# One fused instruction for norm scaling and mask, a newly planned order, and eight output combinations in a row at the end

## The chip, the cores and the metric

The kernel runs on one core of a Trainium2 chip. The metric is device time in microseconds. A core has five engines that work side by side: TensorE (PE in the profile, its weight loads PEld) for matrix products, VectorE (DVE), ScalarE (ACT) and GpSimd (POOL) for everything else, and SyncE (SP), which here only issues transfers to the 16 DMA engines. Each engine runs its own instructions strictly in program order, so an instruction that waits holds up all behind it on that engine.

## The reference

Attention with a compressive memory feeds a soft mixture of experts (B = H = 8, S = 576, D = 64; 4,608 tokens of width 512; 32 slots, 8 experts):

```
scores = q @ k.T / 8, causal mask;  a = softmax(scores);  local = a @ v
q_p = phi(q)                                     # elu(q) + 1
mem_out = (q_p @ M_prev) / (q_p @ z_prev + 1e-6)
x = g * mem_out + (1 - g) * local                # g = sigmoid(beta), per head
logits = x @ phi;  d = softmax(logits, over tokens);  c = softmax(logits, over slots)
slot_out = relu((d.T @ x) @ w1) @ w2             # per expert
out = c @ slot_out
```

## The kernel before

**Pairs of heads.** Attention runs over 32 pairs (8 batches by 4 pairs of heads, 128 partitions hold two heads). Every step of a pair is a small function `op_*`; the text `SEQ` lists some 2,500 of them as `name@pair` and is the order of the program on all engines at once: each engine gets its instructions in the order in which `SEQ` comes to them. `EV` says for each copy or elementwise step which engine does it (`a` ACT, `v` DVE, `p` POOL). A digit behind a colon names the PSUM bank (`psT0` to `psT3`, or `psS0`, `psS1`) that the step takes; a step that takes a bank waits until the last reader of that bank's content before is done.

**Steps of one pair that the change or the prediction touch.** `s4 s3 s2 s1` are score products into psS (L399), `sa` a small one (L418), `max.*` adds the mask and takes row maxima on DVE (L469), `exp.*` is ACT's exponential (L478), `t.*`, `tf`, `ta` are transposes of the weights into psT (L565, L571, L575), `te.*`, `tfe`, `tae` evict them, `av.*` and `ava` multiply with v (L603, L610), `u4` adds the first block and the memory product (L624 to L629).

**Two round trips through DRAM in every pair.** The softmax sums: `rec` (DVE, L483 and L484) inverts them, `rt` transposes, `rte` copies, `rrw` writes them to DRAM (`rs<-rts`), `rrr` reads them back spread over 64 partitions (`rm<-rs`, two transfers of 144 KB, L504), and `mo` and `xa` (DVE, L643, L654) need them; `mo`, `xm`, `xa` are also the last readers of the three psT banks of the pair's output. The memory norm: `norm` (PE), `neps` scales the 128x144 result out of PSUM, `nmk` multiplies by a 0/1 mask, `nred` sums and inverts (L538), `nrw` and `nrr` go through DRAM (`rb<-rd`), `qn` multiplies q_p by it (L554), and `u4` needs that.

**Weights.** 64 tiles of 512 KB. `w@0` to `w@28` have places of their own and are loaded between pairs; `w@29` to `w@46` go to places that attention frees (`WORD`, `FREE`); the last 17 are loaded over the first ones while the experts run. All transfers but two small ones are issued by SP, in the order of `SEQ`.

**After attention.** The `y` steps finish token 512 of every batch and the slot softmax. `fl.n` are filler products on the identity whose result nobody reads. Then, no longer by `SEQ`, come the experts: `f1` and `f1t` (first layer), `f2(0, ...)` (left half of the output columns), `piece` (a sixteenth of the right half's second layer, 8 PE instructions), `g1` and `g2` (normalise and spread a half), `c1` and `c2` (combination weights of the last two token groups), and `comb(half, group)`: 4 products in two psP buffers (of three), one half evicted by ACT and the other by DVE, and a 512 KB store issued by SP. 18 combinations give the output.

Of the kernel before, what the change touches and what calls it, by code (L numbers as in the profile page):

```python
# [28 lines left out]
loadq@1 qhi@0 kn@0 loadm@0 qlo@0 loadk@1 qrelu@0 kl@0 gate@0 s4@0:01 max.40@0 qexp@0 max.41@0 exp.40@0 qphi@0 fl.2@0:0  # L29
s3@0:0 exp.41@0 s1@0:1 max.30@0 s2@0 norm@0:0 qhi@1 max.20@0 sa@0 max.10@0 t.4b@0:1 neps@0 qlo@1 loadk@2 kn@1 loadm@1  # L30
nmk@0 max.21@0 loadq@2 exp.30@0 loadv@0 max.a@0 kl@1 nred@0 te.4b@0 max.11@0 exp.a@0 nrw@0 max.31@0 exp.21@0 qrelu@1
fl.4@0:2 s4@1:01 exp.20@0 exp.31@0 t.2@0:2 max.41@1 exp.10@0 ta@0:3 t.3@0:0 qexp@1 max.40@1 t.4a@0:1 exp.11@0 tae@0
s3@1:0 qphi@1 te.3@0 te.2@0 nrr@0 s2@1:1 rec@0 te.4a@0 s1@1 rt@0:3 max.10@1 kn@2 qhi@2 t.1@0:0 rte@0 max.11@1 exp.10@1
norm@1:2 rrw@0 kl@2 max.20@1 sa@1 te.1@0 tf@0:1 max.30@1 exp.41@1 loadk@3 av.0@0:3 max.a@1 loadq@3 max.21@1 qlo@2
exp.11@1 neps@1 ava@0:0 exp.40@1 max.31@1 av.1@0 nmk@1 tfe@0 av.3@0 qn@0 s4@2:01 exp.20@1 rrr@0 nred@1 exp.31@1 u4@0:2
max.40@2 exp.21@1 nrw@1 w@0 max.41@2 exp.30@1 av.2@0 loadm@2 qrelu@2 exp.a@1 s3@2:0 loadv@1 rec@1 qexp@2 rt@1:1 s2@2:1
qphi@2 rte@1 exp.41@2 rrw@1 s1@2 xa@0 sa@2 mo@0 kn@3 t.2@1:1 nrr@1 t.3@1:0 max.10@2 qhi@3 te.2@1 t.1@1:3 xm@0 w@1 te.3@1
kl@3 loadq@4 t.4a@1:1 loadk@4 te.1@1 max.31@2 norm@2:2 exp.10@2 max.21@2 t.4b@1:0 te.4a@1 neps@2 rrr@1 qlo@3 tf@1:3
max.a@2 te.4b@1 max.20@2 ta@1:2 max.11@2 av.0@1:1 exp.21@2 max.30@2 nmk@2 tae@1 exp.40@2 nred@2 s4@3:01 exp.a@2 qn@1
nrw@2 exp.20@2 av.3@1 max.41@3 w@2 av.2@1 exp.11@2 ava@1:0 tfe@1 exp.30@2 av.1@1 max.40@3 exp.41@3 u4@1:2 exp.40@3  # L40
s1@3:0 xa@1 qrelu@3 loadm@3 exp.31@2 s3@3:1 loadv@2 max.11@3 nrr@2 exp.11@3 s2@3 rec@2 mo@1 rt@2:3 kn@4 t.3@2:0 max.31@3
t.2@2:1 qhi@4 rte@2 te.3@2 xm@1 t.1@2:3 rrw@2 kl@4 qexp@3 sa@3 ta@2:0 max.20@3 t.4a@2:2 te.1@2 loadk@5 max.21@3 tae@2
t.4b@2:3 te.2@2 qphi@3 tf@2:0 te.4a@2 max.10@3 qlo@4 exp.20@3 norm@3:1 max.30@3 av.0@2:2 exp.10@3 max.a@3 neps@3 rrr@2
exp.31@3 nmk@3 s4@4:01 te.4b@2 qn@2 nred@3 exp.30@3 av.2@2 max.41@4 nrw@3 tfe@2 loadq@5 av.3@2 av.1@2 w@3 max.40@4
exp.a@3 exp.21@3 ava@2:1 u4@2:3 exp.40@4 rec@3 rt@3:0 mo@2 qrelu@4 loadv@3 s1@4:0 rte@3 exp.41@4 s2@4 rrw@3 s3@4:1
max.11@4 xa@2 loadm@4 t.4a@3:0 nrr@3 xm@2 qexp@4 sa@4 ta@3:2 x3.0@0:1 max.10@4 loadk@6 tae@3 max.a@4 tf@3:3 max.20@4
x3e.0@0 t.3@3:2 qhi@5 tfe@3 t.1@3:1 te.4a@3 qlo@5 rrr@3 te.3@3 t.2@3:3 te.1@3 x3.1@0:0 te.2@3 kn@5 t.4b@3:2 qphi@4
av.0@3:1 te.4b@3 kl@5 max.30@4 exp.11@4 loadq@6 ava@3:3 max.31@4 norm@4:2 av.3@3 neps@4 av.2@3 qn@3 exp.a@4 av.1@3
exp.30@4 max.21@4 nmk@4 u4@3:2 exp.20@4 nred@4 exp.31@4 s4@5:01 exp.10@4 mo@3 qrelu@5 loadv@4 loadm@5 exp.21@4 nrw@4
xa@3 t.4b@4:1 max.41@5 x1.0@0:3 te.4b@4 xm@3 qexp@5 t.4a@4:1 max.40@5 ta@4:2 x1.1@0 tae@4 qphi@5 s3@5:0 x1l@0 te.4a@4  # L50
x1m@0 s2@5:1 x3e.1@0 rec@4 nrr@4 s1@5 x1e@0 max.30@5 t.3@4:2 kn@6 max.10@5 rt@4:3 sa@5 te.3@4 x2@0:1 qhi@6 rte@4 t.2@4:0
x2a@0 exp.10@5 rrw@4 max.20@5 t.1@4:3 qlo@6 te.2@4 max.11@5 tf@4:2 max.31@5 te.1@4 loadk@7 x4.0@0:0 loadq@7 tfe@4 x2m@0
kl@6 w@4 norm@5:3 exp.41@5 ava@4:2 neps@5 av.0@4:1 max.21@5 exp.31@5 x4a.0@0 x3.2@0:3 nmk@5 exp.40@5 rrr@4 max.a@5
nred@5 x3.3@0:0 x3e.2@0 s4@6:01 qn@4 nrw@5 exp.30@5 x3e.3@0 exp.11@5 u4@4:3 max.40@6 exp.21@5 exp.a@5 av.1@4 qrelu@6
exp.20@5 loadm@6 w@5 max.41@6 qexp@6 av.2@4 av.3@4 exp.41@6 qphi@6 s1@6:0 loadv@5 s2@6 nrr@5 rec@5 x2e@0 s3@6:1 mo@4
rt@5:0 xa@4 qhi@7 sa@6 t.1@5:1 rte@5 xm@4 t.3@5:2 kn@7 rrw@5 te.1@5 max.31@6 ta@5:0 t.2@5:3 te.3@5 kl@7 max.11@6 loadk@8
t.4a@5:1 te.2@5 max.10@6 loadq@8 t.4b@5:2 max.21@6 te.4a@5 tf@5:3 max.30@6 te.4b@5 qlo@7 norm@6:1 max.20@6 exp.11@6
av.0@5:2 max.a@6 exp.20@6 tae@5 neps@6 rrr@5 exp.30@6 nmk@6 s4@7:01 qn@5 nred@6 exp.10@6 exp.31@6 tfe@5 av.2@5 nrw@6
ava@5:0 exp.21@6 max.40@7 av.1@5 exp.40@6 max.41@7 av.3@5 u4@5:1 exp.a@6 x2s@0 exp.41@7 s1@7:0 qrelu@7 rec@6 loadv@6
exp.40@7 s3@7:1 loadm@7 max.11@7 mo@5 exp.11@7 s2@7 nrr@6 rt@6:3 xa@5 kn@8 t.1@6:2 xm@5 t.2@6:0 qhi@8 rte@6 te.1@6  # L60
t.4a@6:3 rrw@6 max.31@7 te.2@6 qlo@8 ta@6:1 sa@7 max.10@7 t.3@6:2 qexp@7 tae@6 loadk@9 max.21@7 tf@6:0 w@6 te.4a@6
max.a@7 t.4b@6:1 qphi@7 te.3@6 x4.1@0:3 te.4b@6 max.20@7 norm@7:2 exp.10@7 max.30@7 av.0@6:1 tfe@6 rrr@6 kl@8 exp.30@7
x5@0:0 neps@7 s4@8:01 x4a.1@0 exp.31@7 nmk@7 x5e@0 qn@6 nred@7 exp.a@7 av.1@6 exp.21@7 max.41@8 nrw@7 exp.20@7 ava@6:2
loadq@9 av.3@6 max.40@8 av.2@6 u4@6:3 rec@7 exp.40@8 rt@7:0 mo@6 qrelu@8 loadm@8 s2@8:0 rte@7 loadv@7 rrw@7 xa@6 s3@8:1
s1@8 nrr@7 t.3@7:0 max.10@8 xm@6 qexp@8 t.2@7:1 t.4a@7:2 te.3@7 max.21@8 sa@8 max.11@8 x3.0@1:3 te.2@7 te.4a@7 tf@7:0
x3e.0@1 t.1@7:1 qphi@8 rrr@7 tfe@7 t.4b@7:2 max.31@8 te.1@7 w@7 x3.1@1:3 loadq@10 kn@9 max.a@8 ta@7:0 max.30@8 av.0@7:1
x3e.1@1 te.4b@7 kl@9 qhi@9 norm@8:3 exp.11@8 av.1@7 neps@8 qn@7 exp.10@8 av.3@7 av.2@7 tae@7 nmk@8 max.20@8 exp.31@8
u4@7:23 qlo@9 nred@8 exp.20@8 nrw@8 exp.41@8 ava@7 w@8 mo@7 qrelu@9 s4@9:01 loadk@10 exp.21@8 loadv@8 xa@7 loadm@9
exp.30@8 xm@7 x1.0@1:0 max.41@9 x1.1@1 t.4b@8:1 max.40@9 x1l@1 exp.a@8 t.4a@8:3 qexp@9 x1m@1 ta@8:2 nrr@8 s2@9:0 qphi@9
x1e@1 w@9 s1@9 rec@8 te.4a@8 s3@9:1 max.20@9 tae@8 te.4b@8 rt@8:0 x1d@0 x2@1:3 max.11@9 kn@10 tf@8:2 qhi@10 rte@8 x2m@1  # L70
t.1@8:1 rrw@8 kl@10 exp.11@9 x2a@1 t.3@8:0 max.30@9 te.1@8 t.2@8:3 max.21@9 te.3@8 sa@9 qlo@10 max.10@9 norm@9:1 te.2@8
max.31@9 x4.0@1:0 exp.41@9 neps@9 av.0@8:3 max.a@9 nmk@9 exp.10@9 qn@8 exp.30@9 rrr@8 x3.3@1:1 nred@9 tfe@8 s4@10:01
x3e.3@1 exp.40@9 nrw@9 w@10 u4@8:21 loadk@11 max.41@10 exp.31@9 loadq@11 x4a.0@1 exp.20@9 av.2@8 max.40@10 loadm@10
exp.a@9 av.3@8 x2e@1 ava@8 qrelu@10 exp.21@9 av.1@8 qexp@10 rec@9 sa@10:0 x3.2@1:0 loadv@9 exp.40@10 qphi@10 nrr@9
s1@10:1 x3e.2@1 mo@8 s3@10 s2@10 xm@8 rt@9:0 kn@11 t.4a@9:3 max.a@10 rte@9 max.21@10 t.2@9:2 rrw@9 te.4a@9 max.20@10
t.3@9:0 qhi@11 te.2@9 max.30@10 norm@10:3 qlo@11 loadq@12 te.3@9 xa@8 t.1@9:2 loadk@12 exp.a@10 neps@10 w@11 tf@9:0
max.10@10 te.1@9 max.11@10 t.4b@9:1 kl@11 max.31@10 exp.41@10 ta@9:3 av.0@9:2 te.4b@9 exp.31@10 rrr@9 tae@9 nmk@10 tfe@9
exp.11@10 s4@11:01 qn@9 exp.30@10 nred@10 ava@9:1 exp.10@10 max.40@11 av.1@9 nrw@10 exp.20@10 max.41@11 av.3@9 av.2@9
exp.21@10 x2s@1 u4@9:3 exp.40@11 exp.41@11 rec@10 s1@11:0 qrelu@11 loadv@10 s3@11:1 loadm@11 max.11@11 mo@9 exp.11@11
s2@11 nrr@10 ta@10:0 xa@9 kn@12 sa@11 t.4a@10:2 xm@9 qhi@12 tae@10 rt@10:1 qexp@11 t.1@10:0 max.30@11 qlo@12 tf@10:3  # L80
rte@10 te.1@10 max.a@11 max.31@11 rrw@10 t.3@10:1 te.4a@10 t.2@10:0 max.20@11 te.3@10 qphi@11 t.4b@10:2 loadk@13 te.2@10
x4.1@1:1 kl@12 tfe@10 norm@11:0 exp.20@11 max.21@11 av.0@10:3 exp.31@11 max.10@11 neps@11 rrr@10 x1d@1 s4@12:01
exp.21@11 te.4b@10 nmk@11 qn@10 exp.10@11 x4a.1@1 ava@10:0 exp.30@11 nred@11 av.2@10 av.3@10 max.41@12 exp.a@11 av.1@10
# [1050 lines left out]
```

## Time and profile before

| | |
|---|---|
| time, median of 3 runs | 452.92 us (452.63 to 454.46) |
| profiled execution, its own time | 454.92 us |
| its span (first to last instruction) | 453.1 us |
| mean granted TensorE clock | 0.984 |
| PE, DVE, ACT, POOL busy | 426.6, 344.5, 333.0, 152.9 us |
| moved by DMA | 97.42 MB, mean 215 GB/s |

The busy time of an engine is an average over stages with different limits. An idle time of PE is read together with what ended it: the profile names the engine, line and tile that released the waiting instruction, and from there one goes back along that engine to the transfer or instruction that was late.

### The profile page before, as it was taken

How to read it: one execution, taken by the hardware profiler on the slowest of the kernel's cores; microseconds unless marked ns; L12 is line 12 of the kernel's file. 1: busy time of each engine (PE TensorE's matmuls, PEld its weight loads, DVE VectorE, ACT ScalarE, POOL GpSimd, SP SyncE). 2: the span in 40 equal slices, each digit the busy share in tenths (PEclk: the TensorE clock that was granted, in tenths of full speed). 3: DMA queues.
4: the chain of work that ended last, by engine and by line, in shares of the span. 5: the costliest groups of instructions: out<-in, count | busy, mean ns of one | idle time of the engine just before them, and what ended most of it. 6: DMA issues, size and time to landing. Idle time of an engine off the chain costs nothing.

```text
span 453.1 us, 12442 instructions
## 1 busy us (share of the span) xinstructions
PE 426.6 (94%) x4364; PEld 283.2 (62%) x4364; DVE 344.5 (76%) x1200; ACT 333.0 (73%) x947; POOL 152.9 (34%) x165
## 2 busy tenths in 40 slices
...
GB/s 157 146 251 196 195 117 248 163 214 247 225 194 193 215 161 208 214 196 169 273 185 220 159 157 232 153 139 201 186 169 128 89 317 297 352 359 412 243 327 291
DMA packets 65710, 97.42 MB, mean 215 GB/s; under 512 B 14704, under 2 KB 41072, under 8 KB 65648
## 3 DMA queue, kind: packets, MB, share of 16 engines
...
q10 hardware_dynamic: 288, 0.09, 0.1%
...
## 4 chain that ended last, share of the span: by engine, by line
PE 67%; DVE 12%; DMA 9%; ACT 5%; issue 3%; POOL 1%; SPq 1%; DVEq 0%; ACTq 0%; POOLq 0%
PE psS L399 12%; PE psT L603 12%; PE psT L565 12%; DMA rm<-rs 7%; PE psT L624 5%; DVE P L469 4%; PE psT L727 4%; PE pf L966 3%; PE pf L949 3%; PE pp L1011 2%; PE psT L571 2%; PE psT L522 2%; ACT P L478 2%; ACT at L333 2%; PE psT L666 2%
## 5 line engine op out<-in xcount | busy, mean ns | idle before, releaser
L478 ACT ACTIVATE P<-P,nm 128x320 f32<-128x320 f32 (+4 forms) x288 | 166.2, 587 | 9.4 <-DVE nm L469 8.7
L469 DVE CUSTOM_DVE_ANT_0 P<-psS,mq 128x192 f32<-128x192 f32 (+3 forms) x256 | 133.6, 548 | 11.0 <-PE psS L399 9.8
L333 ACT COPY at<-psT 128x512 f32<-128x512 f32 (+1 forms) x187 | 94.4, 553 | 29.1 <-PE psT L565 10.3
L565 PE MATMUL psT<-cs,P 128*128 128x128 f32 x640 | 89.0, 281 | 4.5 <-DVE xt L654 2.5
L399 PE MATMUL psS<-K,X 64*128 64x288 f32 (+3 forms) x960 | 88.3, 319 | 4.1 <-DVE nm L469 3.2
L399 PEld LDWEIGHTS psS<-K,X 64*128 64x128 f32 x960 | 69.2, 185 | 26.0 <-issue 7.5
L603 PE MATMUL psT<-at,mq 128*64 128x256 f32 (+3 forms) x512 | 83.5, 443 | 0.6 <-ACT P L478 0.4
L565 PEld LDWEIGHTS psT<-cs,P 128*128 128x128 f32 x640 | 72.9, 144 | 10.4 <-issue 5.5
L478 ACT ACTIVATION_READ_ACCUMULATOR P<-P,nm 128x1 f32 x288 | 57.3, 199 | 0.0
L385 POOL TENSOR_TENSOR X<-mq,X 128x512 fp32r<-128x512 f32 x31 | 40.8, 1315 | 24.2 <-DVE X L336 10.7
L391 POOL TENSOR_TENSOR K<-kq,K 128x576 fp32r<-128x576 f32 x27 | 38.6, 1429 | 10.1 <-DVE nm L469 5.3
L603 PEld LDWEIGHTS psT<-at,mq 128*64 128x64 f32 x512 | 28.9, 136 | 18.4 <-issue 9.5
L624 PE MATMUL psT<-kq,m 64*64 64x512 f32 x64 | 34.2, 614 | 0.9 <-POOL kq L554 0.8
L643 DVE TENSOR_TENSOR xt<-psT,rm 128x448 f32<-128x448 f32 (+7 forms) x60 | 23.8, 435 | 13.8 <-DMA rm<-rs 7.8
L625 PE MATMUL psT<-at,mq 64*64 64x512 f32 x64 | 34.2, 615 | 0.0
L627 PE MATMUL psT<-kq,m 64*64 64x512 f32 x64 | 34.2, 615 | 0.0
L626 PE MATMUL psT<-at,mq 64*64 64x512 f32 x64 | 34.2, 615 | 0.0
L338 POOL TENSOR_SCALAR X<-mq 128x512 fp32r<-128x512 f32 x21 | 13.0, 619 | 52.9 <-PE psT L489 20.9
L336 DVE COPY at<-psT 128x512 f32<-128x512 f32 (+2 forms) x45 | 25.0, 563 | 4.5 <-PE psT L565 3.1
L338 POOL TENSOR_SCALAR K<-kq 128x576 fp32r<-128x576 f32 x17 | 11.7, 691 | 48.3 <-PE psS L399 39.6
L509 POOL TENSOR_SCALAR kq<-mq 128x576 f32<-128x576 f32 x22 | 14.8, 674 | 39.0 <-PE psT L629 36.5
L516 DVE SCALAR_TENSOR_TENSOR kq<-mq,kq 128x576 f32<-128x576 f32 x32 | 26.0, 814 | 2.3 <-ACT mq L512 2.2
(198 smaller groups left out, 686.7 us busy)
## 6 DMA issues: line engine op xcount, KB each, us to landing
...
```

The source lines that it names most:

```text
L333: nc.scalar.copy(o, i)
L385: ALU_ENG[ev("qlo", n)].tensor_tensor(out=X[:, 1, :], in0=st[n]["q"][:, 64:576], in1=X[:, 0, :].bitcast(F32), op=ALU.subtract)
L391: ALU_ENG[ev("kl", n)].tensor_tensor(out=K2[:, 1, :], in0=st[n]["k"][:, 0:S], in1=K2[:, 0, :].bitcast(F32), op=ALU.subtract)
L399: nc.tensor.matmul(out(h), X[ROW[h], x, 128 * i - 128:128 * i], K2[ROW[h], y, o + k0:o + k1], start=(x, y) == (0, 0), stop=(x, y) == (0, 1))
L469: nc.vector.tensor_tensor_reduce(out=sm, in0=src, in1=msk, op0=ALU.add, op1=ALU.min, scale=-0.125, scalar=3.0e38, accum_out=s["nm"][:, J:J ...
L478: nc.scalar.activation(sm, sm, AF.Exp, scale=-1.0, bias=s["nm"][:, J:J + 1], accum_out=s["sum"][:, J:J + 1])
L565: nc.tensor.transpose(out=ps[:, 256 * x + 128 * h:256 * x + 128 * h + 128], in_=chunk(n, i, h, c), identity=ident)
L603: nc.tensor.matmul(s["oa"][ROW[h], 512 - w:512], vt[:, c, ROW[h]], at[:, base + 512 * h:base + 512 * h + w], start=first, stop=s["parts"] ...
L624: nc.tensor.matmul(om[ROW[0], :], s["m"][ROW[0], 0:64], s["qp"][ROW[0], 64:576], start=True, stop=True)
L625: nc.tensor.matmul(w2(s["oa"][ROW[1], :]), vt[ROW[0], 4, ROW[1]], af[ROW[0]], start=first, stop=s["parts"] == 5)
L626: nc.tensor.matmul(w2(s["oa"][ROW[0], :]), vt[ROW[1], 4, ROW[0]], af[ROW[1]], start=first, stop=s["parts"] == 5)
L627: nc.tensor.matmul(om[ROW[1], :], s["m"][ROW[1], 0:64], s["qp"][ROW[1], 64:576], start=True, stop=True)
```

## The change

Three things change.

1. **Norm.** `nmk` is gone. Its mask and the gate factor are multiplied once at the start into a small table `mg`, and `neps` becomes one DVE instruction for all 32 pairs that adds 1e-6 and multiplies by `mg`. Before, `neps` was on ACT in 12 pairs and on DVE in 20, `nmk` on POOL in 24 and on DVE in 8.
2. **Order.** `SEQ`, `EV` and `WORD` are new throughout. Beside it `EV` moves seven evictions of 512 columns from DVE to ACT, POOL takes five casts `qhi` more, and the fillers shrink from 13 units (`fl.2 fl.4 fl.5 fl.1 fl.1`) to 7 (`fl.2 fl.1 fl.2 fl.1 fl.1`).
3. **Last phase.** `c1` and `c2` move up between the first-layer products; `comb(0, 0)` to `comb(0, 7)` stand in a row, then 13 pieces in a row, then `comb(0, 8)`.

```
     def op_neps(n):
         rn = st[n]["rn"] = sml.tile([128, 144], F32, name="rn", bufs=1)
-        if ev("neps", n) == "a":
-            nc.scalar.activation(rn, st[n]["nps"][:, 0:144], AF.Identity, bias=epg[:, n % NP:n % NP + 1], scale=gc[:, n % NP, 9:10])
-        else:
-            nc.vector.tensor_scalar(out=rn, in0=st[n]["nps"][:, 0:144], scalar1=1e-6, scalar2=gc[:, n % NP, 9:10], op0=ALU.add, op1=ALU.mult)
-    def op_nmk(n):
-        rn = st[n]["rn"].rearrange("a (u x) -> a u x", x=9)
-        ALU_ENG[ev("nmk", n)].tensor_tensor(out=rn, in0=rn, in1=maskn.rearrange("a (u o) -> a u o", o=1).broadcast_to([128, 16, 9]), op=ALU.mult)
+        nc.vector.scalar_tensor_tensor(out=rn.rearrange("a (u x) -> a u x", x=9), in0=st[n]["nps"][:, 0:144].rearrange("a (u x) -> a u x", x=9), scalar=1e-6,
+                                       in1=mg[:, n % NP].rearrange("a (u o) -> a u o", o=1).broadcast_to([128, 16, 9]), op0=ALU.add, op1=ALU.mult)
...
     f1(0, 0)
     f1(0, 1)
     f1t(0, 0)
+    c1(7)
     f1(1, 0)
     f1t(0, 1)
+    c1(8)
     f1(1, 1)
     f1t(1, 0)
+    c2(7)
     f2(0, 0, 0)
     f1t(1, 1)
+    c2(8)
...
     g2(0)
-    c1(7)
     piece(1)
-    comb(0, 0)
-    comb(0, 1)
-    c1(8)
-    piece(2)
-    comb(0, 2)
...
-    comb(0, 6)
-    piece(3)
+    for t4 in range(NQ - 1):
+        comb(0, t4)
+    piece(13)
     g1(1)
-    comb(0, 7)
+    comb(0, NQ - 1)
     g2(1)
-    comb(0, 8)
```

SP's queue early in attention, before: what stands ahead of and behind the `rm<-rs` of pair 1 (`w_` tiles are weights, `mq<-in_q` and `kq<-in_k` the inputs of pair 4, `mq<-in_v` values, `rb<-rd` the norm's way back).

```order
L499 DMA rs<-rts 4x128 x2
L500 DMA rs<-rts 2x1x64
L550 DMA rb<-rd 64x4x144 x2
L769 DMA w_474<-in_w_dram 128x1024
L361 DMA mq<-in_q_dram 128x704
L366 DMA kq_103<-in_k_dram 128x640
L504 DMA rm<-rs 64x576 x2
L544 DMA rd<-rq 128x9
L769 DMA w_552<-in_w_dram 128x1024
```

The same place now:

```order
L493 DMA rs<-rts 4x128 x2
L494 DMA rs<-rts 2x1x64
L537 DMA rb<-rd 64x4x144 x2
L355 DMA mq<-in_q_dram 128x704
L498 DMA rm<-rs 64x576 x2
L360 DMA kq_103<-in_k_dram 128x640
L531 DMA rd<-rq 128x9
```

The weight ahead of this transfer and the one behind it are gone from here (the first weight now comes in pair 3), and the k load stands behind it.

SP's queue around the `rm<-rs` of pair 17, before:

```order
L366 DMA kq_103<-in_k_dram 128x640
L769 DMA w_3482<-in_w_dram 128x1024
L361 DMA mq<-in_q_dram 128x704
L504 DMA rm<-rs 64x576 x2
L544 DMA rd<-rq 128x9
L769 DMA w_3549<-in_w_dram 128x1024
L769 DMA w_3551<-in_w_dram 128x1024
```

Around that of pair 20, now:

```order
L355 DMA mq<-in_q_dram 128x704
L360 DMA kq_104<-in_k_dram 128x640
L756 DMA w_4040<-in_w_dram 128x1024
L498 DMA rm<-rs 64x576 x2
L531 DMA rd<-rq 128x9
L756 DMA w_4098<-in_w_dram 128x1024
L756 DMA w_4101<-in_w_dram 128x1024
```

In the new order pair 17 has no weight just ahead of its `rm<-rs`, and pair 20 has the set that pair 17 had: one weight, one q and one k load ahead, two weights behind.

PE at the last pair, before: the products with v, five filler units on `cs` (the identity; each row of `x5` is five units), then `u4`.

```order
L603 MATMUL psT_6053<-at,mq 64x512 x2
L610 MATMUL psT_6061<-at,mq 64x64 x2
L603 MATMUL psT_6053<-at,mq 64x384 x2
L355 MATMUL psS_6070<-cs 128x256 x5
L624 MATMUL psT_6076<-kq_104,m 64x512
```

And now:

```order
L590 MATMUL psT_6020<-at,mq 64x512 x2
L597 MATMUL psT_6028<-at,mq 64x64 x2
L590 MATMUL psT_6020<-at,mq 64x384 x2
L590 MATMUL psT_6020<-at,mq 64x128 x2
L349 MATMUL psS_6038<-cs 128x256 x2
L611 MATMUL psT_6041<-kq_104,m 64x512
```

Two filler units are left of five, and one more product with v stands ahead of them.

## Rows read from the trace of the kernel before

**Rows 1.** The page, part 1: busy us, share of the span, instructions.

```profile
PE 426.6 (94%) x4364; PEld 283.2 (62%) x4364; DVE 344.5 (76%) x1200; ACT 333.0 (73%) x947; POOL 152.9 (34%) x165
```

**Rows 2.** Stretches: start:end, us, busy of each engine (instructions), PEclk, DMA share, GB/s.

```profile
0.00:46.00 46.00, 39.53 (x328) 25.89 (x330) 32.96 (x120) 35.51 (x99) 18.03 (x25) 1.00 0.63 188
46.00:356.00 310.00, 304.52 (x3118) 210.39 (x3118) 272.11 (x978) 264.56 (x768) 130.90 (x138) 0.99 0.65 190
356.00:394.00 38.00, 34.74 (x378) 24.41 (x378) 20.79 (x67) 18.52 (x54) 4.00 (x5) 0.96 0.80 276
394.00:420.00 26.00, 25.87 (x303) 10.93 (x298) 3.83 (x7) 2.85 (x6) 0.00 (x0) 1.00 0.99 381
420.00:453.00 33.00, 21.91 (x253) 11.58 (x253) 14.81 (x29) 11.58 (x23) 0.00 (x0) 0.88 0.84 291
```

**Rows 3.** Timeline of PE: start, us, instruction, [idle before <-releaser].

```profile
34.98 0.64 PE L624 MATMUL psT<-kq,m 64*64 64x512 f32 x1 [0.77 <-POOL kq L554]
...
39.54 0.70 PE L399 MATMUL psS<-K,X 64*128 64x320 f32 x6 [2.22 <-DVE nm L469]
...
222.34 0.63 PE L565 MATMUL psT<-cs,P 128*128 128x128 f32 x4 [1.34 <-DVE xt L643]
...
372.11 0.63 PE L565 MATMUL psT<-cs,P 128*128 128x128 f32 x4 [2.55 <-DVE xt L654]
```

**Rows 4.** Timeline of DVE: first uses of the spread softmax sums.

```profile
38.73 0.23 DVE L654 TENSOR_TENSOR xt<-psT,rm 128x64 f32<-128x64 f32 x1 [3.99 <-DMA rm<-rs]
...
186.05 0.76 DVE L643 TENSOR_TENSOR xt<-psT,rm 128x256 f32<-128x256 f32 x2 [1.42 <-DMA rm<-rs]
...
221.43 0.76 DVE L643 TENSOR_TENSOR xt<-psT,rm 128x192 f32<-128x192 f32 x2 [1.40 <-DMA rm<-rs]
```

**Rows 5.** Timeline of SP: issues of transfers (start, us spent issuing).

```profile
30.64 2.19 SPq L504 DMA_DIRECT2D rm<-rs  x2
...
180.15 1.14 SPq L504 DMA_DIRECT2D rm<-rs  x2
...
214.65 1.12 SPq L504 DMA_DIRECT2D rm<-rs  x2
...
363.65 1.51 SPq L504 DMA_DIRECT2D rm<-rs  x2
...
436.65 0.37 SPq L1013 DMA_DIRECT2D out_dram<-P  x1
```

**Rows 6.** Stretches behind the wait at 222, columns as in group 2.

```profile
223.00:226.50 3.50, 3.50 (x20) 3.46 (x19) 3.50 (x13) 2.55 (x5) 0.23 (x1) 0.53 0.52 111
```

**Rows 7.** Groups of DVE, ACT and POOL: xcount | busy us, mean ns | idle before us <-releasers.

```profile
L538 DVE TENSOR_REDUCE rq<-rn 128x9 f32<-128x144 f32 x32 | 13.5, 421 | 8.1 <-POOL rn L534 8.0
L529 DVE TENSOR_SCALAR rn<-psT,rm 128x144 f32<-128x144 f32 x20 | 7.3, 363 | 1.0 <-PE psT L522 0.8
...
L534 DVE TENSOR_TENSOR rn<-rn,rm 128x144 f32<-128x144 f32 x8 | 2.4, 303 | 0.0
```

**Rows 8.** Timeline of PE and DVE ahead of the last pair's u4.

```profile
378.45 0.76 DVE L554 TENSOR_TENSOR kq<-kq,rb 128x576 f32<-128x576 f32 x1 [2.30 <-DMA rb<-rd]
...
379.72 2.43 PE L355 MATMUL psS<-cs 128*128 128x256 f32 x10
```

**Rows 9.** Timeline of PE in the last phase (L966 products, L1011 combinations).

```profile
430.94 1.50 PE L966 MATMUL pf<-w,at 128*32 128x256 f32 x24
...
436.64 2.69 PE L1011 MATMUL pp<-xk,cT 32*128 32x256 f32 x24 [0.30 <-DVE P L336]
439.52 2.69 PE L1011 MATMUL pp<-xk,cT 32*128 32x256 f32 x24 [0.19 <-DVE P L336]
```

**Rows 10.** Stretches of the last phase, columns as in group 2.

```profile
422.00:434.00 12.00, 11.99 (x163) 5.54 (x163) 6.65 (x14) 4.37 (x10) 0.00 (x0) 1.00 0.87 300
434.00:438.00 4.00, 3.40 (x36) 2.07 (x34) 2.42 (x4) 2.42 (x6) 0.00 (x0) 1.00 0.85 294
438.00:451.00 13.00, 4.77 (x44) 3.00 (x44) 4.21 (x7) 3.50 (x6) 0.00 (x0) 0.77 1.04 360
```

433 lines of the change are left out of this document (209 added, 224 removed).

## The prediction

> **What bounds the kernel now.** I read the page first, then a table of stretches, then the waits of PE, and from each wait back to what was late. The page says that PE is busy 94% of the span and DVE 76% [rows 1]. The stretches say where [rows 2]. In the long middle of attention, 46 to 356 us, PE is busy 304.5 of 310 us and DVE 272.1: PE sets the pace, DVE comes behind it with 12% to spare, ACT is like DVE, and POOL is busy for less than half. The start (0 to 46) loses 6.5 us of PE, and the end of attention (356 to 394) 3.3. The experts (394 to 420) keep PE full. In the last 33 us PE is idle for 11, and the DMA engines write: 360 GB/s from 438 on [rows 10].
>
> So a change of the order is worth what it does to PE's few idle times, and to nothing else in attention. The large ones stand in the timeline [rows 3]: 0.77 and 2.22 us near 35 and 39, 1.34 at 222, 2.55 at 372. The last two and the 2.22 have one cause, which DVE's timeline shows [rows 4]: DVE stands 3.99 us at 38.7 and 1.40 at 221.4 for `rm<-rs`, the way back of the softmax sums. While it waits, the row maxima behind it are not taken, or the psT banks of the finished pair are not free, and PE stands. The reader should see how long that way back takes from its issue to its first use: 30.64 to 38.73 is 8.1 us, 214.65 to 221.43 is 6.8, and 180.15 to 186.05 is 5.9 [rows 4, 5]. The third has one weight tile of 512 KB just ahead of it in SP's queue and costs PE almost nothing; the first two have one ahead and one or two behind, with inputs among them. The last one (363.65 to the end of PE's wait at 372.11) has two weights just ahead of it.
>
> **The change part by part.**
>
> *Norm.* Twelve `neps` come to DVE at 0.363 us (the old DVE form, which also reads PSUM), eight `nmk` of 0.303 leave it [rows 7]: 4.4 less 2.4, DVE gains 1.9 us of work in all. The new form has no row; it is nearest to the old `neps`, since both write 144 columns from PSUM. Its bounds are nothing more than that row and 0.67, both old instructions together: 32 x 0.3 = 10 us more on DVE. The seven evictions that move to ACT take more off DVE than the norm adds. What `nmk` cost as a wait stands in the sum's row: DVE was idle 8.0 us for POOL's `rn` [rows 7]. I cost all this at nothing: in the middle PE covers it, being busy 304.5 of 310 while DVE has 38 us free [rows 2]. Without that cover it is between 8.0 less 1.9, a gain of 6.1, and a loss of 10. A gain is capped too: PE's idle time in the middle is 5.5 us.
>
> *The order at pair 1.* The weight ahead of `rm<-rs` and the one behind go, and the k load moves behind it; what is left is lighter than at 180.15, where 5.9 us were enough. I take the waits of 0.77 (for `qn`, whose `rb<-rd` shares that queue) and 2.22 as gone: -3.0 us. Bounds: nothing gained if only the place moves, and -4 if DVE's whole 3.99 counts.
>
> *Pairs 17 and 20.* Pair 17's wait cost 1.34 us, and behind it the granted clock is 0.53 over 3.5 us, mostly 1.2 GHz where it had been 2.4 [rows 3, 6]; at half speed that is some 1.65 us of work lost, together 3.0. In the new order pair 17 has no weight just ahead. But pair 20 has exactly pair 17's set: k, q and a weight ahead, two weights behind, and on PE almost the same products stand between its `rrr` and the bank that `mo` frees (scores, products with v, `u4`; one small `sa` more). I take 3.0 away and put 3.0 back: 0, bounds -3.0 and +1 (pair 8 has a weight, k and q ahead as well and a little less work to cover them).
>
> *The end of attention.* Pair 30 now has three weights ahead of its `rm<-rs`, not two, and the third waits for a place that the transposes of the pair free. Behind `rrr` PE has less to do than before: a `t` (0.63 us for four transposes [rows 3]) and an `x4` of eight products, which I take alike, have moved ahead of it. So 2.55 us grow by some 1.2: +1.2, bounds 0 (if the queue moves faster) and +3.
>
> *Fillers.* Five units before the last `u4` took 2.43 us, and `qn`, for which they might bridge, had ended at 379.2, before they began [rows 8]. Three of five go: -1.5 us, if `qn` is as early again; bounds 0 and -2. The others that go stand at the start, where PE waits for DVE anyway.
>
> *Last phase.* In 422 to 434 PE is busy 11.99 of 12.00, so combinations among pieces hide their evictions; in a row (434 to 438) it is busy 3.40 of 4.00 [rows 10], and three combinations take 2.88 us, start to start [rows 9]. Eight in a row are 7.7 us, 15% of it waits: 1.2 us lost. A piece takes 0.50 (24 instructions in 1.50 [rows 9]) and 13 of them 6.5, as before. `g2`'s copy on ACT, some 0.4 us, is no longer covered by a combination. The four transposes of `c1` and `c2` only move. So the first right-hand store, issued at 436.65 [rows 5], comes up to 1.6 later. For the end it is the queue that counts: 3.6 and 1.2 MB are moved from 422 to 438 [rows 10], 9 of the 18 stores of 0.52 MB, and the other nine take 13 us at 360 GB/s. In the new order the first eight are fed at one per 0.96 us, sooner than 360 GB/s takes them (1.46 each), so they are out by 434; then the queue runs dry while 13 pieces run, and nine stores are left at about 438.2. So +0.3. Bounds: +1.6, and -2.7 if the queue never ran dry (16 us at 360 GB/s are 5.8 MB and not 4.8).
>
> **The sum.** -3.0 + 0 + 1.2 - 1.5 + 0.3 = -3.0 us. The profiled execution took 454.92 us, 453.1 of it span, and lies 2.0 above the median of the runs, 452.92; I carry the difference over: 449.9 us.
>
> **The rivals.**
>
> *The stalls are not put back.* The new order spaces transfers so that neither pair 20 nor pair 30 waits longer than the third case above: -3.0 more at pair 20. For it: weights are now absent from the first pairs and the queue's mean is 190 GB/s in the middle [rows 2]. Against: those weights must come somewhere, and pairs 8, 13, 14 and 20 now hold one or two. 446.9 us, chance 0.18.
>
> *Clock.* PE gets six filler units less, and a further stretch at 1.2 GHz follows, at the end of attention or when the experts begin: 1.65 us each by the same step as at pair 17, 451.6 us with one. For it: after 1.34 us of waiting the clock did fall [rows 3, 6]. Against: after the waits of 0.77 and 2.22 near 35 it did not, the mean over 0 to 46 is 1.00 [rows 2]. Chance 0.13. The Trainium skill, TensorE: Matmul & The Clock Gate, Part 1, says that the throttled state is the default and that activity releases it, which speaks against taking products away that keep PE busy; the trace agrees in the fall behind pair 17, and no row shows a fall for want of fillers.
>
> *No change.* PE sets the pace, and a new order with the same products finds new waits for those removed: the sum's gain of 3.0 at pair 1 comes back at other pairs, say 3.0 at pair 22, which has a weight and a k load ahead and two us of work less to cover them than now. 452.9 us, chance 0.18.
>
> *Slower: DVE waits for the norm product.* `neps` now stands on DVE in all pairs, ahead of row maxima that free the score banks. Where it comes up before PE has done `norm`, maxima and then PE wait. The old `neps` on DVE waited 1.0 us in 20 [rows 7], 0.05 each, which speaks against it; that ACT took twelve of them speaks for it, since ACT's wait held up no maximum. At 0.25 us a pair it costs 8.0, and the sum becomes +5.0: 457.9 us. It turns the sign at 0.09 a pair and is slower by half a per cent from 0.17. Chance 0.16.
>
> **How the numbers follow.** The forecast has 0.35, the rivals 0.18, 0.13, 0.18 and 0.16. Half a per cent, about what a measurement of this kernel can tell from no change, is 2.3 us: 450.7 and 455.2 are the limits. The forecast's own range, from its bounds taken one at a time, is 447 to 452; three quarters of it lie below 450.7. Faster: 0.18 + 0.26 and a little of the clock's case, 0.47. Slower: 0.16 and some of the no-change case, 0.20. Same: the rest, 0.33. The range reaches from 446, a little below the first rival, to 455.5, which leaves out most of the last.
>
> **What would show it.** In the changed kernel's profile: no wait of DVE over 1.5 us for `rm<-rs` before 50 us, and PE idle less than 3 us in total in the first 46; a wait of some 1.4 us at pair 20, near 255, with the clock at 0.5 behind it, and none at pair 17; a wait over 3 us before the last pair's transposes; DVE's wait for `rn` gone and its wait before `neps` not above 2 us in 32; f1 beginning some 3 us earlier than at 394; 8 combinations in about 7.7 us, a hole in the stores before the right half, and the time from the first f1 to the end the same within 0.5. The prediction is wrong if the middle changes by more than 3 us, which none of its terms explains, or if the last phase gains because the queue does not run dry.

## The result: slower by 1.1%

The changed kernel took 458.69 us in the median of five executions (456.69 to 461.53), beside 454.46 (452.63 to 454.86) for five of the kernel before on the same chip. The ratio is 1.0114, 95% interval 1.0066 to 1.0162: slower, by less than 2% but clear of no change, where 449.9 was forecast. Ratios here and below leave out disturbed executions, so a ratio can differ from the quotient of two medians, which are over all. The profiled execution of the changed kernel took 460.05 us, span 458.1.

### The profile page after: what moved, and what is told of

Its sections match the earlier page's. It is cut to its first block, busy times and chain, and to the rows that moved or that the text cites. A ratio compares the mean times of both kernels' runs of the same rounds, so it can differ in the third digit from the quotient of the medians.

```text
span 458.1 us, 12415 instructions
## 1 busy us (share of the span) xinstructions
PE 424.2 (93%) x4352; PEld 280.6 (61%) x4352; DVE 341.7 (75%) x1195; ACT 331.3 (72%) x937; POOL 148.2 (32%) x148
## 4 chain that ended last, share of the span: by engine, by line
PE 63%; DMA 16%; DVE 13%; ACT 3%; issue 2%; SPq 1%; POOL 1%; DVEq 0%; ACTq 0%; POOLq 0%
PE psT L590 12%; PE psS L393 11%; PE psT L552 11%; DMA rm<-rs 8%; PE psT L611 5%; DVE P L463 4%; PE pf L953 3%; PE pf L936 3%; PE psT L714 3%; DMA rs<-rts 2%; PE pp L998 2%; PE psT L558 2%; DMA rd<-rq 2%; PE psT L516 2%; DVE xt L630 2%
## 5 line engine op out<-in xcount | busy, mean ns | idle before, releaser
L472 ACT ACTIVATE P<-P,nm 128x448 f32<-128x448 f32 (+4 forms) x288 | 166.0, 582 | 9.7 <-DVE nm L463 7.9
L326 ACT COPY at<-psT 128x512 f32<-128x512 f32 (+1 forms) x193 | 97.6, 554 | 34.1 <-PE psT L552 22.5
L590 PE MATMUL psT<-at,mq 128*64 128x128 f32 (+3 forms) x512 | 82.9, 442 | 0.0
L472 ACT ACTIVATION_READ_ACCUMULATOR P<-P,nm 128x1 f32 x288 | 55.8, 194 | 0.0
L385 POOL TENSOR_TENSOR K<-kq,K 128x576 fp32r<-128x576 f32 x27 | 40.1, 1486 | 17.9 <-ACT K L326 8.7
L379 POOL TENSOR_TENSOR X<-mq,X 128x512 fp32r<-128x512 f32 x29 | 39.1, 1348 | 13.6 <-DVE at L329 6.6
L331 POOL TENSOR_SCALAR X<-mq 128x512 fp32r<-128x512 f32 x26 | 16.3, 625 | 69.8 <-PE psS L393 24.1
L503 POOL TENSOR_SCALAR kq<-mq 128x576 f32<-128x576 f32 x24 | 16.2, 673 | 53.6 <-PE psT L616 50.7
L541 POOL TENSOR_TENSOR kq<-kq,rb 128x576 f32<-128x576 f32 x16 | 23.5, 1471 | 19.4 <-DMA rb<-rd 16.1
L331 POOL TENSOR_SCALAR K<-kq 128x576 fp32r<-128x576 f32 x19 | 13.2, 695 | 47.3 <-PE psS L393 35.2
```

The lines of the kernel that those rows point to most:

```text
L326: nc.scalar.copy(o, i)
L379: ALU_ENG[ev("qlo", n)].tensor_tensor(out=X[:, 1, :], in0=st[n]["q"][:, 64:576], in1=X[:, 0, :].bitcast(F32), op=ALU.subtract)
L385: ALU_ENG[ev("kl", n)].tensor_tensor(out=K2[:, 1, :], in0=st[n]["k"][:, 0:S], in1=K2[:, 0, :].bitcast(F32), op=ALU.subtract)
L472: nc.scalar.activation(sm, sm, AF.Exp, scale=-1.0, bias=s["nm"][:, J:J + 1], accum_out=s["sum"][:, J:J + 1])
L590: nc.tensor.matmul(s["oa"][ROW[h], 512 - w:512], vt[:, c, ROW[h]], at[:, base + 512 * h:base + 512 * h + w], start=first, stop=s["parts"] ...
```

## The profile after

First part of the page, then the stretches (start:end, us, busy time of each engine, PEclk, DMA share, GB/s). Line numbers are those of the changed kernel, 6 to 13 less than before; in the experiments they are each kernel's own.

```profile
PE 424.2 (93%) x4352; PEld 280.6 (61%) x4352; DVE 341.7 (75%) x1195; ACT 331.3 (72%) x937; POOL 148.2 (32%) x148
0.00:46.00 46.00, 41.25 (x346) 26.74 (x346) 34.99 (x125) 35.92 (x101) 20.34 (x25) 1.00 0.56 160
46.00:356.00 310.00, 297.31 (x3055) 204.31 (x3051) 263.93 (x953) 258.50 (x746) 120.61 (x117) 1.00 0.67 192
356.00:396.00 40.00, 35.60 (x388) 24.83 (x391) 22.98 (x78) 22.32 (x64) 6.20 (x6) 0.96 0.75 246
396.00:422.00 26.00, 26.00 (x298) 11.64 (x294) 6.91 (x22) 3.43 (x8) 1.06 (x1) 1.00 1.00 396
422.00:458.00 36.00, 24.09 (x288) 13.12 (x280) 12.94 (x20) 11.08 (x20) 0.00 (x0) 0.88 0.85 286
```

Against [rows 2]: PE did 1.7 us more in the first 46 us, so the start did get better. Then it was idle for 12.7 us of the 310 in the middle, where it had been idle for 5.5: 7.2 lost. The timeline of PE shows at which waits:

```profile
29.52 0.63 PE L552 MATMUL psT<-cs,P 128*128 128x128 f32 x4 [1.01 <-DVE xt L642]
...
50.04 0.63 PE L552 MATMUL psT<-cs,P 128*128 128x128 f32 x4 [0.97 <-DVE xt L630]
...
76.99 0.28 PE L483 MATMUL psT<-cs,r 128*9 128x128 f32 x1 [1.62 <-DVE r L478]
...
79.38 0.33 PE L552 MATMUL psT<-cs,P 128*128 128x128 f32 x1 [0.80 <-DVE xt L634]
...
181.33 0.27 PE L562 MATMUL psT<-cs,P 128*64 128x128 f32 x1 [2.19 <-DVE xt L641]
...
194.25 0.98 PE L552 MATMUL psT<-cs,P 128*128 128x128 f32 x7 [0.61 <-DVE xt L634]
...
377.20 0.65 PE L552 MATMUL psT<-cs,P 128*128 128x128 f32 x4 [3.03 <-DVE xt L630]
```

These belong to pairs 0, 2, 4 (two), 13, 14 and 30. Those of pairs 2 to 14 are 6.2 of the 12.7 us; the rest is in waits of 0.84 at most, for copies, casts, row maxima and M. None was among the waits of before [rows 3] but the last, and pair 17's 1.34 is gone. Behind most stands the way back of the softmax sums, as before. (The first weight comes earlier than the section on the change says: it is issued at 41.40, between pair 2's write at 39.92 and its read at 42.88.) DVE's timeline at pairs 4 and 13, and what SP issued at pair 13:

```profile
75.02 0.23 DVE L641 TENSOR_TENSOR xt<-psT,rm 128x64 f32<-128x64 f32 x1 [1.68 <-DMA rm<-rs]
...
180.43 0.76 DVE L630 TENSOR_TENSOR xt<-psT,rm 128x256 f32<-128x256 f32 x2 [2.92 <-DMA rm<-rs]
```

```profile
167.95 0.60 SPq L493 DMA_DIRECT2D rs<-rts  x2
168.60 0.60 SPq L494 DMA_DIRECT2D rs<-rts  x1
169.30 1.29 SPq L537 DMA_DIRECT2D rb<-rd  x2
170.63 1.08 SPq L756 DMA_DIRECT2D w<-in_w_dram  x2
171.82 0.36 SPq L355 DMA_DIRECT2D mq<-in_q_dram  x1
172.28 1.11 SPq L498 DMA_DIRECT2D rm<-rs  x2
```

At pair 13 two weights and a q load stand ahead of the read: 8.1 us from 172.28 to the first use, as at pair 1 before [rows 4, 5], and 12.5 from the write's issue. At pair 4 no weight stands there and the read took 4.8 us or less, yet DVE waited 1.68: in this order it comes to the use 3.2 us behind the issue.

A single execution can mislead here. `old_last` (below) runs the same attention again, and its profile says which waits come back: PE stands 1.11 us at pair 4, 1.81 at pair 13 and 2.73 at pair 30. Pair 14's does not, and pair 8, with two weights near its way, costs 1.77 in its place.

The clock, the norm and the last phase, by windows and by group:

```profile
223.00:227.00 4.00, 4.00 (x44) 2.79 (x41) 3.75 (x17) 3.69 (x12) 1.41 (x3) 1.00 0.99 340
377.00:381.50 4.50, 4.30 (x24) 4.27 (x24) 2.10 (x6) 1.17 (x2) 0.00 (x0) 0.62 0.42 151
L520 DVE SCALAR_TENSOR_TENSOR rn<-psT,rm 128x144 f32<-128x144 f32 x32 | 9.6, 302 | 4.2 <-PE psT L516 4.1
426.00:434.00 8.00, 7.32 (x84) 4.16 (x88) 4.75 (x8) 3.93 (x7) 0.00 (x0) 1.00 0.86 292
398.40:458.10 59.70, 47.69 (x553) 22.94 (x552) 18.56 (x37) 14.51 (x28) 0.00 (x0) 0.93 0.91 329
```

The stretch at half speed near 223 [rows 6] is gone, one behind the last long wait remains (0.50 from 373.4 to 376.8 us before). The new norm takes 0.302 us and waits 4.2 us in 32 for its product. From the first f1 to the end pass 59.7 us, beside 59.3.

So the loss is made in attention: the last score product ends at 365.22 (361.14 before), f1 begins at 398.41 (393.87). For these two executions the account closes: 1.7 won up to 46 us, 7.2 lost in the middle, of which 1.65 comes back with the half-clock stretch that went, makes 3.9 of the 4.1; the end of attention adds 0.5 and the last phase 0.5. In three more profiles of the old order (`last_only`, `fl_only`, `norm_only`) the last score product ends at 359.4 to 361.9, in one more of the new (`old_last`) at 363.1, so in these six the new order is always later, by 1.2 to 5.9 us.

## The experiments

Medians are over all executions of a kernel; "before" in the same calls had 454.0 to 455.5.

**Which part of the change.** `norm_only`: before, with the one-instruction norm and no `nmk`.

```diff
-        nc.vector.tensor_scalar(out=rn, in0=..., scalar1=1e-6, scalar2=gc[...], op0=ALU.add, op1=ALU.mult)   # or ACT; then nmk
+        nc.vector.scalar_tensor_tensor(out=rn..., in0=..., scalar=1e-6, in1=mg[...], op0=ALU.add, op1=ALU.mult)
```

> The order and the last phase of before; only the norm is changed: the masked scaling in one DVE instruction that reads PSUM, no nmk, all 32 neps on DVE. Theory Q (queue: the changed kernel lost its time because loads stand ahead of rm<-rs at other pairs than before, so the norm costs nothing): within 1.5 us of before, DVE's wait for the norm product below 3 us in 32. Theory N (norm: DVE stands for the norm product with row maxima behind it): 3 to 5 us slower than before, with a wait of DVE before neps of 4 us or more in all. The prediction's term was 0, with bounds -6.1 and +10.

Measured: 454.81, ratio 1.000 (0.9964 to 1.0037). DVE waited 4.0 us for the product, more than theory Q's 3 and as much as theory N asked for, and it cost nothing. Theory N falls in the order of before.

`last_only`: before, with the changed last phase (the part of the diff behind `SEQ`).

> The order and the norm of before; only the last phase is changed (both transposes of the last combination weights ahead, eight left combinations in a row, 13 pieces, the ninth behind). Prediction's term: +0.3 us (bounds +1.6 and -2.7), first f1 to the end of the span within 0.5 us of before's 59.3. Theories Q and N say nothing against it. A rival: the hole in the stores costs as much as the nine stores run sooner, +1.5 us or more.

Measured: 454.51, ratio 1.001 (0.998 to 1.004), 59.7 us from f1 to the end. The term holds as far as it can be told: with the old last phase this stretch took 59.3 to 60.1 us in ten profiles, 59.6 on average, with the new one 59.7 to 59.9 in eight, 59.8 on average (the two kernels without weights left out).

`old_last`: the changed kernel with the last phase of before.

> The changed kernel with the last phase of before: the new order and the new norm alone. If the loss is in attention (Q, N, or the order of computation, theory C), 457 to 459 us, as the changed kernel; if the last phase were the cause, 453 to 454.

Measured: 459.92 (453.16 to 465.67), ratio 1.0057 (1.0014 to 1.0101). The loss is there without the new last phase: all of it by the medians, half by the ratio, whose interval overlaps that of the whole change. With `norm_only` and `last_only` at no change, that points at the order.

**What in the order: the queue ahead of the read?** `loads_behind`:

```diff
- ... rrw@13 nrr@13 w@13 w@14 loadq@16 rrr@13 nrw@14 ...
+ ... rrw@13 nrr@13 rrr@13 w@13 w@14 loadq@16 nrw@14 ...
```

> The changed kernel; in pairs 0 to 30 each load of q, k or a weight that stood between the two ways of the softmax sums (write rs<-rts, read rm<-rs) is put just behind the read; nothing else moves. Theory Q: the ways from issue to first use fall to 4.5 us or less in all pairs, DVE's idle time for rm<-rs falls from 9.2 us to below 4, the waits of PE at pairs 13 and 14 (2.19 and 0.61) go, and the time falls by 3 us or more, to 452 to 455. Theories N and C (the order of the instructions on PE, DVE and POOL): the ways get shorter but the time stays within 1.5 us of the changed kernel's 458.7. It can also get slower if a load that comes later is then waited for (q or k of the next pairs).

Measured: 461.45, ratio 1.0129 (1.0084 to 1.0174): no gain, and theory Q in this simple form falls. PE's waits at pairs 13, 14 and 30 for `xt` went, as Q said. But what was put behind the read stood ahead of the next pair's M, v and write, and PE now waited for the first two (timeline of PE):

```profile
126.15 0.45 PE L508 MATMUL psT<-kq,m 128*32 128x144 f32 x8 [1.45 <-DMA m<-in_M_dram]
...
384.39 1.08 PE L582 MATMUL psT<-at,mq 128*64 128x512 f32 x4 [3.06 <-DMA mq<-in_v_dram]
```

**Without the weights, without the wait.** `now_before`, `now_after` load one tile in place of 27; `norr_before`, `norr_after` let nobody wait for the sums.

```diff
     def op_w(x):
+        if 0 < x < 27: wt[order[x]] = wt[order[0]] ...
...
-in1=rr[:, 64 + c0:64 + c1]
+in1=gc[:, 0, 0:1].broadcast_to([128, c1 - c0])
```

> The kernel before, with 26 of the 27 weight tiles that are loaded into places of their own during attention left out: the first tile's values stand in for them, so the experts' part is computed with wrong weights, and attention runs with half of its weight traffic or less. Read by the start of f1 (393.9 before). Theory Q (the ways of the softmax sums are long because weights share the queue): the ways at pairs 1 and 17 fall from 8.1 and 6.8 us to 5 or less, PE's waits of 2.22 and 1.34 go, f1 starts 4 us sooner. Theory K (what decides is how much other work the order puts between the read's issue and its first use): the long ways get shorter, f1 starts 3 to 5 us sooner too; the two theories part in the next kernel.

> The same omission in the changed kernel (f1 at 398.4 there). Theory Q: all that the new order lost goes, f1 starts within 1 us of the same omission in the order of before. Theory K: pairs 13 and 30 gain as their ways get shorter, but the waits at pairs 4, 23 and 27, where a way of 4.4 to 4.8 us meets 3.1 us of other work, stay in part, and f1 starts 2 us or more behind that of the kernel before with the same omission. Theory C (the rest of the order: norm, POOL's work, maxima): f1 stays 4 us or more behind.

> The kernel before, where the products that use the way back of the softmax sums read a constant column in its place (the values are wrong); the sums are still written and read back, but nobody waits for them. DVE's idle time for rm<-rs (11.7 us before) is gone. PE's waits of 2.22, 1.34, 0.74 and 2.55 go with it: f1 4 to 6 us sooner, total 448 to 451.

> The same in the changed kernel. Theories Q and K: the waits of 1.01, 0.97, 1.62 with 0.80, 2.19, 0.61, 0.62 and 3.03 go, f1 8 to 10 us sooner, within 1 us of the same omission in the order of before, so that the whole loss lies in the wait for the sums. Theory C: the new order stays 3 us or more behind.

Measured: without weights 453.23 and 453.17; the last phase is some 6 us longer in both, so f1 tells more: 384.34 and 386.48. The weights cost the old order 9.5 us up to f1, the new one 11.9, and 2.1 of the 4.5 between them are left. Both theories had put that too low (3 to 5). The 2.1 rest on one profiled execution each, the first 1.4 us below its median and the second 1.2 above, so they don't choose between the theories; the medians are level, which leaves nothing of the loss. Without the wait for the sums 448.80 and 451.92, ratios 0.9884 (0.9839 to 0.9928) and 0.9923 (0.9876 to 0.9971). The medians are 3.1 apart and the intervals overlap, so whether a part of the loss lies outside the wait for the sums is not settled. Where it might lie: PE waits for v instead (new order, timeline of PE, in the longest of ten executions):

```profile
375.94 1.11 PE L590 MATMUL psT<-at,mq 128*64 128x512 f32 x4 [3.12 <-DMA mq<-in_v_dram]
```

**The prediction's own terms, one at a time.** `moved_before` takes away from the kernel before what the prediction thought gone at pairs 1 and 17; `fl_only` takes three fillers.

```diff
- nrw@1 w@0 ... nrr@1 w@1 loadq@4 loadk@4 rrr@1        - ... loadk@20 w@19 loadq@20 rrr@17
+ nrw@1 ... nrr@1 loadq@4 rrr@1 loadk@4                + ... loadk@20 loadq@20 rrr@17      (w@0, w@1, w@19 behind rrr@2, @3, @21)
...
-fl.5.s@0:0
+fl.2.s@0:0
```

> The kernel before with four loads moved and nothing else: the weight tiles ahead of and behind rm<-rs of pair 1 go behind the reads of pairs 2 and 3, the k load behind pair 1's read, the weight ahead of pair 17's read behind that of pair 21. It tests the prediction's terms for pairs 1 and 17 alone. If they were right and nothing is put back: -3.0 for pair 1, -1.34 for pair 17's wait and -1.65 for the half clock behind it, f1 at 388 and not 394, total 448 to 450. Theory S (any order near this tightness meets the same transfers again elsewhere; a way that is a little late is made up for by one that comes next): 452 to 454.

> The kernel before with two filler products and not five ahead of the last u4. The prediction's term: -1.5 us (bounds 0 and -2). Against it: PE waits for qn there anyway, as in two of the executions profiled since (0.84 to 0.92 us ahead of the same u4), so that the fillers fill a wait: 0 to -0.6.

Measured: 455.13, ratio 1.0001 (0.9961 to 1.0041), and 453.55, ratio 0.999 (0.9958 to 1.0023). The profile of `moved_before` shows the terms come true and be taken back: pair 4's scores begin at 42.62 and not 45.74, pair 20's at 224.59 and not 229.12; then pair 22, with one weight more behind pair 21's read, waits longer than before (PE 0.74, DVE 2.56, a wait that the prediction's list left out), and the clock falls behind it. Timelines of PE and DVE, DVE's of the kernel before, and a window:

```profile
278.93 0.63 PE L563 MATMUL psT<-cs,P 128*128 128x128 f32 x4 [2.54 <-DVE xt L646]
```

```profile
278.03 0.76 DVE L635 TENSOR_TENSOR xt<-psT,rm 128x128 f32<-128x128 f32 x2 [4.37 <-DMA rm<-rs]
```

```profile
280.76 0.76 DVE L643 TENSOR_TENSOR xt<-psT,rm 128x128 f32<-128x128 f32 x2 [2.56 <-DMA rm<-rs]
```

```profile
280.00:284.00 4.00, 4.00 (x23) 3.94 (x23) 2.50 (x9) 2.78 (x7) 0.00 (x0) 0.57 0.46 140
```

Pair 25 begins 1.2 us earlier than before, where pair 24 had been 4.5 ahead. This execution is 2.4 us below the kernel's median, so what is left of the lead in it is not a gain. In `fl_only` the time from the last score product to f1 falls from 32.73 to 30.82 us, 0.67 of it by a shorter wait of the transposes: 1.2 for three fillers. Two other profiles with all five (`last_only`, `norm_only`) give 1.6 and 0.9 by the same step, and the total can't tell any of it from nothing.

**A queue of their own for the weights.** `wq_before`, `wq_after`.

```diff
-            nc.sync.dma_start(out=t, in_=w1[...])
+            (nc.scalar if x < 27 else nc.sync).dma_start(out=t, in_=w1[...])
```

> The kernel before with the 27 weight tiles that have places of their own issued on ACT's queue and not SP's (same places in the order). Theory Q: the small ways no longer stand behind a weight in their own queue; the ways at pairs 1 and 17 fall to 5 us or less, f1 comes 3 to 6 us sooner. Against it (theory B, what is shared is the engines that move the bytes and not the queue): the ways stay above 6 us and the time within 1.5 us.

> The same in the changed kernel. Theory Q: the ways of pairs 13 and 30 fall from 8 us to 5, f1 comes 4 to 7 us sooner than 398.4, total 452 to 455. Theory B: within 1.5 us of the changed kernel.

Measured: 462.35, ratio 1.0201 (1.014 to 1.0261), and 471.58, ratio 1.0407 (1.0345 to 1.0468). Neither theory said so: it is much worse. At pair 17 of the old order (DVE's timeline, SP's and ACT's issues, and the page's queues: packets, MB, share):

```profile
230.12 0.76 DVE L643 TENSOR_TENSOR xt<-psT,rm 128x192 f32<-128x192 f32 x2 [6.18 <-DMA rm<-rs]
```

```profile
220.56 0.94 ACTq L769 DMA_DIRECT2D w<-in_w_dram  x2
```

```profile
220.71 1.14 SPq L504 DMA_DIRECT2D rm<-rs  x2
```

```profile
q1 hardware_dynamic: 61472, 82.38, 58.6%
q10 hardware_dynamic: 4176, 14.24, 9.2%
```

The read is issued beside two weights and takes 9.4 us to its first use (6.8 before, with one weight ahead in the same queue); PE stands 6.12 us for it. Elsewhere it is mixed. At pairs 1 and 30 the read came back sooner (6.5 and 5.9 us beside 8.1 and 7.6), as theory Q said; at pairs 0, 2, 6, 7 and 15 DVE waits 2.0 to 3.1 us for sums that it did not wait for before.

Two things beside the queue changed as well: ACT now spends 9.3 us issuing, and a load leaves when ACT comes to it. In the old order PE's waits for ACT did not grow (2.2 us, 2.8 before), but no run holds the moments of issue fixed, so what follows is argued and not shown. A weight takes bytes from a small way that moves beside it, and in one queue the way is shielded from what is issued behind it. For the second half there is a count. Among the waits counted below, 50 have no weight ahead; in 23 of them none is issued within 2.5 us behind the read either, in 27 one or two are. The round trip takes 8.8 us in both, the read 4.9 and 5.3.

The Trainium skill has the first half (DMA: Bandwidth & Descriptors, "Issuing engines are not separate DMA queues"): transfers of all issuing engines run on the same 16 DMA engines and interleave. The trace agrees at pair 17, where the read took 2.6 us more. The same page of the Trainium skill ("Queues, rings and completion order") says that an engine changes between queues packet by packet. The profile's packets are 3.4 KB on average in the weights' queue and 1.3 in SP's; if the page's packets stand in the same proportion, which no run shows, an estimate by that rule gives the weights the larger share. No run here shows the engines' turns themselves.

**The deciding test: exchange the weights' places.** `wB_after` gives the new order the weights' places of before (behind the same other transfer of the same pair), `wA_before` the reverse; `spread_after` and `spread_before` put one weight behind each read of pairs 0 to 28.

```diff
- ... nrr@13 w@13 w@14 loadq@16 rrr@13 ... rrw@14 loadk@17 w@15 w@16 rrr@14 ...
+ ... nrr@13 loadq@16 rrr@13 w@13 ...      rrw@14 loadk@17 rrr@14 w@14 ...            (spread_after)
```

> The changed kernel, in which each of the 29 weight loads into places of their own stands behind the same other transfer of the same pair as in the kernel before; all else as in the changed kernel. Theory W: the new order's loss goes, f1 at 394 and not 398, total 453 to 455. Theory K: 457 to 460, as the changed kernel, with waits at pairs 0, 4, 23, 27 and 30 as there.

> The kernel before, in which the same 29 weight loads stand where they stand in the changed kernel (first one at pair 2, two ahead of the read of pairs 13 and 14, none at pair 1). Theory W: the loss comes along, 457 to 459. Theory K: the order of before has the cover for them, 451 to 455; pair 1's wait of 2.22 goes and f1 may come up to 3 us sooner.

> The changed kernel with one weight load just behind each read of the softmax sums of pairs 0 to 28, so that no pair has two and none stands ahead of its read. Theory W: 451 to 454, the waits at pairs 13 and 14 gone. Theory K: 456 to 459, since the short covers stay.

> The same places in the order of before. Theory W: 450 to 453, within 1 us of spread_after; the waits at pairs 1 and 17 gone. Theory K: 450 to 453 too, 3 us or more ahead of spread_after.

Measured:

| weights' places | order of before | new order |
|---|---|---|
| each order's own | 454.0 to 455.5 | 458.69 (1.0114, 1.0066 to 1.0162) |
| the other order's | 461.00 (1.0118, 1.0065 to 1.0171) | 463.82 (1.0199, 1.0152 to 1.0247) |
| even | 454.18 (1.0007, 0.9977 to 1.0036) | 454.98 (1.0011, 0.9978 to 1.0044) |

With the same even places the orders are level, and the new order's interval lies below the changed kernel's: the loss is in where the weights stand. Both came out some 1 us above theory W's ranges. But a place is good or bad only with the order around it: each order's own places beat the other's by 5 to 7 us in the medians, by 0.9 and 1.2% in the ratios, where for the new order the intervals just touch. Theory W as written falls by half (the new places do bring a loss to the old order, the old places don't cure the new one), theory K (the loss stays in any case) falls too. In `wA_before` pair 13 shows how it goes wrong (timeline of PE, then SP's queue):

```profile
178.72 0.52 PE L557 MATMUL psT<-cs,P 128*128 128x128 f32 x3 [3.14 <-DVE xt L646]
```

```profile
165.42 1.27 SPq L542 DMA_DIRECT2D rb<-rd  x2
166.74 1.07 SPq L761 DMA_DIRECT2D w<-in_w_dram  x2
167.91 0.66 SPq L491 DMA_DIRECT2D rs<-rts  x2
168.62 0.61 SPq L492 DMA_DIRECT2D rs<-rts  x1
169.34 0.36 SPq L358 DMA_DIRECT2D kq<-in_k_dram  x1
169.80 0.36 SPq L353 DMA_DIRECT2D mq<-in_q_dram  x1
174.03 1.14 SPq L496 DMA_DIRECT2D rm<-rs  x2
```

Here the weights stand behind the pair's `rb<-rd`, the transfer they stood behind in the new order, but that is now ahead of the write of the sums: the write, 4.5 KB in all, delays the read's issue to 6.1 us behind it, while the read itself takes 3.8. The way to count is write and read together. In 16 profiles (all but those of the `norr` and `wq` kernels) DVE waited over 0.25 us for the sums of pairs 0 to 30 in 106 cases. From the write's issue to the use passed 8.8 us on average where no weight was issued between 3 us ahead of the write and the read (50 cases, 6.3 to 11.3), 9.3 with one (24), 10.8 with two (26), 11.1 with three (6). These are the cases where DVE came first; of the 32 with two or three weights 15 are pair 30's, so this is a tendency and not a price per weight.

**A version that beats both?** `late_after` and `late_before` start the weights at pair 3; the second also has the new norm and two fillers.

```diff
+ one w behind each of rrr@3 to rrr@28; two behind @11, @15, @19 (late_after), @7, @18, @24 (late_before)
```

> The changed kernel with the 29 weight loads behind the reads of pairs 3 to 28, one each, two at pairs 11, 15 and 19 (behind which the next pair's read has 6 us or more of other work). Theory W: the wait of 2.34 us at pair 0 shrinks to some 0.6, f1 at 388 to 390 and not 390.8, total 451 to 454. Theory K: the order of the start keeps the wait, within 1 us of spread_after's 455.0.

> The order of before with the norm in one instruction, two fillers and not five, and the weight loads behind the reads of pairs 3 to 28, two at pairs 7, 18 and 24. Theory W: no waits over 0.6 us of PE before pair 4, f1 at 387 to 390, total 450 to 453, faster than before by 0.3 to 0.9%. If gains at single places are taken back at others (theory S): 453.5 to 455.

Measured: 453.28, ratio 0.9982 (0.9937 to 1.0026), and 454.08, ratio 1.0009 (0.9963 to 1.0056), before at 455.49. Pair 0's wait in `late_after` fell from 2.34 us in `spread_after` to 0.78, as theory W said; `late_before` lies where theory S had it, its gains taken back. Neither sum is to be told from no change. No version here beats the kernel before.

## Why the prediction was wrong, by its steps

*The failing step: "Pairs 17 and 20 ... I take 3.0 away and put 3.0 back: 0", and with it that nothing else changes in the middle.* Taking away was right: no wait at pair 17, granted clock 1.00 from 223 to 227. Pair 20, named as the one that pays, did not: its read had 5.8 us to the first use, and DVE did not wait for it. Pairs 13 and 14 paid 2.8, pair 4 paid 2.4, pair 2 paid 1.0. In place of 0 the middle cost 7.2 less 1.65, some 5.5 (in these two executions; pairs 4 and 13 pay in `old_last` too, pair 14 does not). Two things were left out. First, the prediction named pairs 13 and 14 as holding one or two weights, in a rival, and gave them no price; an even list of all 32 pairs would have found in pair 13 two weights and a q load ahead of the read, beside the one weight, q and k of pair 1 that went with 8.1 us. Second, it asked how much work covers the way only at pairs with a weight ahead of the read (8, 17, 20, 22, 30). Pair 4 has no weight there and waits, since the new order comes to the use 3.2 us behind the issue; and what stands ahead of the write, of v and of M counts as well (`wA_before`, `loads_behind`).

*Pair 1, -3.0.* Right for the place: `moved_before` shows 3.1 by pair 4 (2.6 to 3.1 against four profiles of the old order). In the changed kernel 1.7 were left at 46 us; pair 0's new wait is 1.01, and PE was idle for 4.75 us of the first 46, where less than 3 were forecast.

*End of attention and fillers, +1.2 and -1.5.* The wait grew by 0.5 (2.55 to 3.03), within its bounds; the fillers give some 1.2 (0.9 to 1.6) where they are removed alone. Together the end came to +0.5 and not -0.3. What took back the rest is not settled; a wait of 0.47 for `xt` at 389.4 is part of it. The base was high as well: in three more profiles of the old order PE waits 1.27 to 1.88 us there and not 2.55.

*Norm, 0.* Right: `norm_only` at 1.000. The instruction costs 0.302 us and not 0.363, DVE's wait for `rn` (8.0 us) is gone, and the wait for the product, 4.2 us in 32, is over the 2 us forecast and costs nothing in the order of before. In the new order it was not tried by itself; that both orders come out level with even weights, one with the old norm and one with the new, leaves little room for the 8 us of the slower rival.

*Last phase, +0.3.* Not contradicted: +0.5 in this trace, +0.2 between the averages of 10 and 8 profiles, the hole in the stores (433.93 to 439.69) where it was put, `last_only` at 1.001.

*The rivals.* "Not put back" falls. The clock's falls: one stretch at half speed in attention, where before had two. "No change" had the mechanism, new waits for those removed, but at pair 22, which did not wait, and at too small a price. The slower rival gave 457.9, near the result, by luck: its mechanism wasn't at work. The test that the prediction set itself ("wrong if the middle changes by more than 3 us") is the one that caught it.

*What stays open.* Why a way with no weight in it takes 6.3 us once and 11.3 another time, whether the waits for v and M carry a part of the loss, and why executions of one kernel lie up to 14 us apart (`late_after`), these runs don't settle.
